# Sums out of a PSUM bank placed one to two slots ahead of the bank's next use, and token sums of a pair begun with its first block

## The chip, the cores and the metric

The kernel runs on one core of one Trainium2 chip, in float32. The metric is device time in microseconds (us), the median over runs. A core has five engines with a queue each: TensorE (PE, matmuls, with PEld for loading weights), VectorE (DVE), ScalarE (ACT), GpSimd (POOL) and SyncE (SP), which here only issues transfers. Each engine works its own queue in order; semaphores make one engine wait for another.

## The reference

Two blocks, one after the other. The first is an attention with sketched features: queries and keys (4 batches x 4 heads x 1088 rows x 32) are each projected twice to 8 values, whose outer product gives 64 features; keys and values are summed into a 64x32 matrix, and queries are multiplied into it and divided by a denominator. Its output, brought to 4352 tokens x 128, is the input `x` of the second block:

```
gate = 1.0 / (1.0 + np.exp(-(x @ w_gate)))      # 4352x128 @ 128x1536
val  = x @ w_val                                # 4352x128 @ 128x1536
out  = gate * val @ w_out                       # 4352x1536 @ 1536x128
```

Most of the arithmetic is in the second block, and the change touches only that.

## The kernel before, in words

The tokens go in chunks: eight of 512 and a last one of 256. Per chunk the 1536 hidden columns go in twelve blocks of 128 (`NJ`); the last chunk takes two blocks at once, so it has six steps. Such a step is a *wave*, made by `w1`: eight matmuls into two PSUM banks for gate and value (`wave`, L477), then ACT takes the sigmoid (`sg`, L485). In the next step `glu` lets DVE multiply value and sigmoid to the hidden block `g` (L507). Two blocks make a pair, `pair`.

The second matmul multiplies `g` with `w_out`. Chunk 0 and the last chunk do it plainly (`w2`, L370). Chunks 1 to 7, where `fast(ci)` holds, use a Strassen-like scheme with seven products instead of eight on a pair (two blocks of 128 hidden columns by two halves of 256 tokens by two halves of 64 outputs). It needs sums of weights, `ws`, made once by GpSimd in two halves (`weight_sums`, the second half called in chunk 1 when its second wave is issued), and for each pair sums of tokens, `tsum` rows t0 to t3, made by GpSimd in `token_sums`.

The products accumulate over the six pairs of a chunk in two banks. `w2_a` puts four of the seven products, a matmul each, into the first bank, `acc0`, and `w2_b` the other three into the second, `acc1`; all are recorded at L339 as `prod`. The lower 64 partitions of each bank are called `lo`, the upper `hi`. After the last pair the outputs must be put together from both banks: ACT copies `hi` to SBUF (`other`, L401 and L435), and DVE adds `lo` and the copies into rows of a tile `res` (all recorded at L412, the line of the helper `add`). Then `res` is transposed in two halves (`turned`, L451) and stored. The sums, by the names of the code:

- first sums: first bank's `lo` plus the first copy, for two rows of `res`
- third: the other half of the first bank's `lo`, plus a row of `res`; after it the first bank is free
- fourth: a row of `res` less the second copy; reads no bank
- fifth and seventh: the two halves of the second bank's `lo`; after them the second bank is free
- last sums: rows of `res` with each other; read no bank

The order of the work is written by hand: the four compute engines run in the order in which the program issues their instructions. `slot` is the loop of that order. One turn of it is a *slot*: it calls `glu` for the wave before, runs the next entry of `moe["late"]` (one list of sums), runs the products that are due from `moe["todo"]`, and issues one wave. Products of a pair are due three slots (`w2_a`) and four slots (`w2_b`) after its second block. So with s the slot of a chunk's last `w2_a`, slot s+1 has the last `w2_b`, slot s+2 the first `w2_a` of the next chunk into the same first bank, and slot s+3 the first `w2_b` into the second. The late sums ran in slots s+1 (first), s+2 (third), s+3 (fourth, fifth, seventh) and s+4 (last sums), each ahead of the products of its slot and behind the `g` of that slot.

Attention work of batches 1 to 3 is placed between slots by number (`plan`, and calls before it): transposes of keys and queries (`kT`, `qT`, `kab`), feature products (`kp`, `qp`), sums (`z`, `zs`) on DVE, small matmuls on PE, and transfers by SP. What SP issues is not in the hand-written order.

Of the kernel before, what the change touches and what calls it, by code (L numbers as in the profile page):

```python
# [8 lines left out]
F32 = mybir.dt.float32  # L9
# [3 lines left out]
ALU = mybir.AluOpType  # L13
# [3 lines left out]
P = 128  # L17
# [3 lines left out]
def kernel(  # L21
# [12 lines left out]
    nc = tc.nc  # L34
# [20 lines left out]
    raw = ctx.enter_context(tc.tile_pool(name="raw", bufs=NJ // 2))  # L55
# [90 lines left out]
    HALF = TCH // 2  # L146
    ws = const.tile([P, 4, NJ // 2, 64], F32, tag="ws", name="ws")
    w_in = {}
# [130 lines left out]
    for c in range(2):  # L279
        rows = slice(64 * c, 64 * c + 64)  # L280
        nc.vector.tensor_reduce(
            out=m_col[rows, c],
            in_=ident[rows].rearrange("p (k j) -> p j k", j=R),
            axis=mybir.AxisListType.X,
            op=ALU.add,
        )
    for t, x in (
# [5 lines left out]
        out=e_sum,  # L293
# [13 lines left out]
    moe = {"sum": -1, "ci": 0, "w": 0, "n": 0, "ready": 0, "acc": None, "gate": None, "todo": [], "late": []}  # L307
# [14 lines left out]
        ):  # L322
            nc.gpsimd.tensor_tensor(out=out, in0=in0, in1=in1, op=op)

    def token_sums(g):
        t = raw.tile([P, 4, HALF], F32, tag="w_in", name="tsum")
        g1 = g[:, 0].rearrange("p (t x) -> p t x", t=2)
        nc.gpsimd.tensor_tensor(  # L328
            out=t[:, :2],
            in0=g.rearrange("p f (t x) -> p t f x", t=2)[:, 1],  # L330
            in1=g1,
            op=ALU.subtract,
        )
        nc.gpsimd.tensor_tensor(out=t[:, 2], in0=t[:, 1], in1=g1[:, 0], op=ALU.add)  # L334
        nc.gpsimd.tensor_tensor(out=t[:, 3], in0=t[:, 2], in1=g[:, 1, :HALF], op=ALU.subtract)  # L335
        return t

    def product(out, lhsT, rhs, start, stop):
        nc.tensor.matmul(  # L339
# [46 lines left out]
    fst = {}  # L386

    def w2_a(ci, i, g, t):
        if i == 0:
            moe["sum"] = ci  # L390
            fst["a"] = pso.tile([P, TCH], F32, tag="acc0", name="prod")
        lo, hi = fst["a"][:64], fst["a"][64:]
        w, first, last = w_sb[:, 2], i == 0, i == NJ // 2 - 1
        product(lo[:, :HALF], w[:, 2 * i, :64], g[:, 0, :HALF], first, last)
        product(hi[:, :HALF], w[:, 2 * i + 1, :64], g[:, 1, :HALF], first, last)
        product(lo[:, HALF:], ws[:, 3, i], g[:, 1, HALF:], False, last)
        product(hi[:, HALF:], ws[:, 1, i], t[:, 2], False, last)
        if last:
            e = fst["e"] = raw.tile([P, 2, 2, HALF], F32, tag="w_in", name="other")[:64]
            r = fst["r"] = raw.tile([P, 5, HALF], F32, tag="w_in", name="res")[:64]  # L400
            nc.scalar.copy(out=e[:, 0], in_=hi.rearrange("p (u x) -> p u x", u=2))  # L401

            def first_sums():
                add(ends(r, 1, 3), twice(lo[:, :HALF]), e[:, 0])

            def third():
                add(r[:, 2], lo[:, HALF:], r[:, 4])

            moe["late"] += [[first_sums], [third]]

    def add(out, in0, in1, op=ALU.add):
        nc.vector.tensor_tensor(out=out, in0=in0, in1=in1, op=op)  # L412

    def twice(x):
        return bass.AP(tensor=x.tensor, offset=x.offset, ap=[list(x.ap[0]), [0, 2], [1, HALF]])

    def ends(r, u, step):
        x = r[:, u]
        return bass.AP(
            tensor=x.tensor, offset=x.offset, ap=[list(x.ap[0]), [step * HALF, 2], [1, HALF]]  # L420
        )

    def w2_b(ci, i, g, t):
        if i == 0:
            fst["b"] = pso.tile([P, TCH], F32, tag="acc1", name="prod")
        lo, hi = fst["b"][:64], fst["b"][64:]
        w, first, last = w_sb[:, 2], i == 0, i == NJ // 2 - 1
        p5 = (lo[:, :HALF], ws[:, 0, i], t[:, 0], first, last)
        p4 = (hi[:, :HALF], w[:, 2 * i + 1, 64:], t[:, 3], first, last)
        p7 = ((hi if i % 2 else lo)[:, HALF:], ws[:, 2, i], t[:, 1], False, i >= NJ // 2 - 2)  # L430
        for p in (p4, p5, p7) if i % 2 else (p5, p4, p7):
            product(*p)
        if last:
            e, r = fst["e"], fst["r"]
            nc.scalar.copy(out=e[:, 1], in_=hi.rearrange("p (u x) -> p u x", u=2))  # L435
            o_sb = sbA.tile([P, 2, TCH // 32, 32], F32, tag="o_sb", name="o_sb")

            def fourth():
                add(r[:, 3], r[:, 4], e[:, 1, 0], op=ALU.subtract)

            def fifth():
                add(ends(r, 2, 2), twice(lo[:, :HALF]), ends(r, 2, 2))

            def seventh():
                add(r[:, 0], lo[:, HALF:], e[:, 1, 1])

            def last_sums():
                add(r[:, 3:5], r[:, 3:5], twice(r[:, 0]))

            def turned(d):  # L450
                nc.vector.transpose(  # L451
                    out=o_sb[:64, d].rearrange("p t x -> p (t x)"),
                    in_=r[:, 1 + 2 * d : 3 + 2 * d].rearrange("p u x -> p (u x)"),
                )

            def turn_store():
                turned(1)
                store(ci, lambda g4: o_sb[32 * (g4 % 2) : 32 * (g4 % 2) + 32, g4 // 2])

            moe["late"] += [[fourth, fifth, seventh], [last_sums], [lambda: turned(0)], [turn_store]]  # L460

    def w1():

        ci = moe["ci"]
        t0, tw = tok_chk[ci]
        jn = TCH // tw
        j0 = moe["w"] * jn
        wv = psm.tile([P, 2, TCH], F32, tag="wave", name="wave")

        tp = tw // 2 if ci == 0 and j0 == 0 else tw  # L470
        turn = (moe["w"] // 2) % 2
        for o in range(0, tw, tp):
            for which in range(2):
                for jj in range(jn):
                    for c in (0,) if ci == 0 else (1 - turn, turn):
                        d = slice(0, P) if ci == 0 else slice(64 * c, 64 * c + 64)
                        nc.tensor.matmul(  # L477
                            out=wv[d, which, jj * tw + o : jj * tw + o + tp],
                            lhsT=w_sb[:, which, j0 + jj, d],
                            rhs=xT[:, t0 + o : t0 + o + tp],  # L480
                            start=True,
                            stop=True,
                        )
        sg = sbG.tile([P, TCH], F32, tag="sg", name="sg")
        nc.scalar.activation(out=sg, in_=wv[:, 0], func=ACTF.Sigmoid)  # L485
        if ci == 0:
            if j0 == 1:
                narrow_01(2, 3)
            if 0 < j0 < NJ - 2:
                narrow_w(j0 + 1, 3)  # L490
            narrow_w(j0 + 2, 1)
            narrow_w(j0 + 2, 2)
            if j0 < 3:
                narrow_w(j0 + 3, 0)
            if j0 > 1:
                narrow_w(j0 + 4, 0)
            if j0 == NJ - 3:
                weight_sums(0, NJ // 4)
        if ci == 1 and j0 == 1:
            weight_sums(NJ // 4, NJ // 2)  # L500
        if moe["w"] % 2 == 0:
            moe["g"] = sbG.tile([P, 2, TCH], F32, tag="g", name="g")
        pair, odd, n = moe["g"], moe["w"] % 2, moe["n"]

        def glu():
            g = pair[:, odd]
            nc.vector.tensor_tensor(out=g, in0=wv[:, 1], in1=sg, op=MUL)  # L507
            todo = moe["todo"]
            if not fast(ci):
                lag = 2 if ci == 0 else 3 if j0 else 4  # L510
                part = (ci, j0, jn, g.rearrange("p (j t) -> p j t", j=jn))
                todo.append((n + lag, lambda: w2(*part)))
            elif odd:
                part = (ci, j0 // 2, pair, token_sums(pair))
                todo.append((n + 3, lambda: w2_a(*part)))
                todo.append((n + 4, lambda: w2_b(*part)))

        moe["gate"] = glu
        moe["w"] += 1
        moe["n"] += 1  # L520
        if j0 + jn == NJ:
            moe["ci"] += 1
            moe["w"] = 0
# [6 lines left out]
    def slot(group, waves):  # L530

        if group is not None:
            group()
        todo = moe["todo"]
        for _ in range(waves):
            more = moe["ci"] < len(tok_chk)
            if more and sum(tok_chk[moe["ci"]]) > moe["ready"]:
                break
            glu()
            for step in moe["late"].pop(0) if moe["late"] else ():  # L540
                step()
            while todo and todo[0][0] <= moe["n"]:
                todo.pop(0)[1]()
            if more:
                w1()
            elif not todo:
                break
            else:
                todo.pop(0)[1]()
# [512 lines left out]
    else:  # L1062
        nc.vector.tensor_copy(
            out=s4[:, 1:],
# [8 lines left out]
        out=st_[:, : 2 * R],  # L1073
# [10 lines left out]
        out=sk,  # L1084
# [6 lines left out]
        op=MUL,  # L1091
# [75 lines left out]
    late = []  # L1167
# [122 lines left out]
```

## Time and profile before

| What | us |
|---|---|
| median of 3 runs | 337.98 |
| lowest and highest | 337.73, 340.97 |
| span of the profiled execution | 340.6 |
| PE busy on `wave` (L477) | 218.3 |
| PE busy on `prod`, four groups at L339 | 65.8 + 35.2 + 26.3 + 25.0 |
| DVE busy on `g` (L507) | 70.0 |
| POOL busy on `tsum` (L328, L334, L335) | 63.1 + 32.5 + 33.0 |

Busy times of PE overlap between groups, since matmuls are pipelined; the sum over groups is more than the engine's 301.0 us. The page cuts the span into 40 slices of 8.5 us and gives each engine's busy share in tenths. Idle time of an engine other than the bounding one costs nothing by itself.

### The profile page before, as it was taken

The numbers are of one execution on the slowest core, as the hardware profiler recorded it, in microseconds if no ns is written. First come the engines' busy times: TensorE is split into PE (matmuls) and PEld (weight loads), VectorE is DVE, ScalarE is ACT, GpSimd is POOL, SyncE is SP. The second block draws the span as 40 slices with busy tenths as digits, with TensorE's granted clock in tenths as the row PEclk, the third lists the DMA queues.
The fourth block names the chain that finished last, engine by engine and source line by source line (L and its number), as shares of the span: only waits on it lengthen the run. The fifth ranks groups of instructions, "written<-read, shape, count | busy, mean of one in ns | idle before, by whom it ended". The sixth has DMA issues, their size and how long they took to land.

```text
span 340.6 us, 5502 instructions
## 1 busy us (share of the span) xinstructions
PE 301.0 (88%) x2176; PEld 158.3 (46%) x2176; DVE 187.4 (55%) x317; ACT 88.8 (26%) x164; POOL 155.7 (46%) x178
## 2 busy tenths in 40 slices
PE   9899998999949997699977998599976997699973
PEld 4534332445524553246634554245633554256842
DVE  6987899865453674357534955247223423243333
ACT  3465422122312223022231224021221223022310
POOL 1565564843633455144452975334560654245300
PEclk9999999999998999899999999989997999899999
DMA  8985135654000665131006630001000200001003
GB/s 223 368 238 135 34 119 147 161 138 140 0 0 2 155 164 133 36 113 17 0 2 152 166 64 2 0 4 30 0 0 2 32 2 0 0 13 20 0 2 46
DMA packets 29689, 24.34 MB, mean 71 GB/s; under 512 B 19616, under 2 KB 24864, under 8 KB 29664
## 3 DMA queue, kind: packets, MB, share of 16 engines
q1 hardware_dynamic: 28752, 23.23, 26.3%
q10 hardware_dynamic: 912, 0.77, 0.9%
q8 instruction: 17, 0.28, 0.4%
q14 instruction: 8, 0.07, 0.1%
HBM read 20.73 MB, written 3.26 MB: 70 GB/s over the span
## 4 chain that ended last, share of the span: by engine, by line
PE 73%; DVE 9%; DMA 8%; POOL 4%; ACT 3%; issue 2%; SPq 1%; DVEq 0%; POOLq 0%
PE wave L477 47%; PE prod L339 19%; DVE g L507 3%; DVE res L412 3%; PE moeout L370 3%; ACT sg L485 3%; DMA v<-in_v_dram 3%; DMA w_in<-in_moe_w_out_dram 2%; DMA bq<-dq 2%; POOL tsum L328 2%; DMA w_in<-in_moe_w_gate_dram 1%; PE nps L1004 1%; POOL head L118 1%; PE kvz L810 1%; POOL tsum L334 1%
## 5 line engine op out<-in xcount | busy, mean ns | idle before, releaser
L477 PE MATMUL wave<-xT,w_sb 128*64 128x512 f32 (+3 forms) x820 | 218.3, 582 | 0.0
L507 DVE TENSOR_TENSOR g<-wave,sg 128x512 f32<-128x512 f32 x102 | 70.0, 687 | 135.7 <-ACT sg L485 135.7
L328 POOL TENSOR_TENSOR tsum<-g 128x512 f32<-128x512 f32 x42 | 63.1, 1503 | 133.2 <-DVE g L507 133.1
L485 ACT ACTIVATE sg<-wave 128x512 f32<-128x512 f32 x102 | 60.9, 597 | 223.8 <-PE wave L477 216.9
L477 PEld LDWEIGHTS wave<-xT,w_sb 128*64 128x64 f32 (+1 forms) x820 | 88.2, 143 | 66.7 <-issue 46.4
L339 PE MATMUL prod<-tsum,ws 128*64 128x256 f32 x252 | 65.8, 392 | 18.9 <-DVE res L412 17.3
L339 PEld LDWEIGHTS prod<-tsum,ws 128*64 128x64 f32 x252 | 31.7, 140 | 36.9 <-issue 26.2
L339 PE MATMUL prod<-g,w_sb 128*64 128x256 f32 x168 | 35.2, 392 | 11.0 <-DVE res L412 11.0
L335 POOL TENSOR_TENSOR tsum<-tsum,g 128x256 f32<-128x256 f32 x42 | 33.0, 785 | 3.3
L334 POOL TENSOR_TENSOR tsum<-tsum,g 128x256 f32<-128x256 f32 x42 | 32.5, 774 | 3.3
L339 PEld LDWEIGHTS prod<-g,w_sb 128*64 128x64 f32 x168 | 16.9, 142 | 32.3 <-issue 30.0
L339 PE MATMUL prod<-tsum,w_sb 128*64 128x256 f32 x84 | 26.3, 396 | 0.0
L339 PE MATMUL prod<-g,ws 128*64 128x256 f32 x84 | 25.0, 379 | 0.0
L118 POOL TENSOR_TENSOR head<-head,tail 128x384 int32<-128x384 int32 (+2 forms) x14 | 13.4, 955 | 18.1 <-DVE head L109 13.9
L370 PE MATMUL moeout<-g,w_sb 128*128 128x512 f32 (+1 forms) x48 | 18.6, 500 | 2.2 <-DVE res L412 1.8
L339 PEld LDWEIGHTS prod<-g,ws 128*64 128x64 f32 x84 | 11.5, 137 | 3.9
L370 PEld LDWEIGHTS moeout<-g,w_sb 128*128 128x128 f32 x48 | 8.5, 189 | 9.9 <-issue 6.1
L339 PEld LDWEIGHTS prod<-tsum,w_sb 128*64 128x64 f32 x84 | 11.0, 140 | 2.9 <-issue 2.3
L668 DVE TENSOR_TENSOR kp<-kab 128x1152 f32<-128x1152 f32 (+2 forms) x10 | 10.7, 1088 | 0.0
L788 DVE TENSOR_TENSOR qp<-qp,bq 128x1152 f32<-128x1152 f32 (+1 forms) x7 | 9.0, 1291 | 2.0 <-DMA bq<-dq 2.0
L451 DVE STREAM_TRANSPOSE o_sb<-res 64x512 f32<-64x512 f32 x14 | 9.6, 688 | 0.0
L127 DVE SCALAR_TENSOR_TENSOR w_sb<-square,head 128x384 f32<-128x384 f32 (+1 forms) x11 | 5.7, 518 | 3.9 <-POOL head L118 3.9
(110 smaller groups left out, 186.6 us busy)
## 6 DMA issues: line engine op xcount, KB each, us to landing
qp<-dq SPq DMA_DIRECT2D x7, 576.0 KB, 5.0
bq<-dq SPq DMA_DIRECT2D x14, 288.0 KB
v<-in_v_dram SPq DMA_DIRECT2D x16, 144.0 KB, 2.7
kq<-in_k_dram SPq DMA_DIRECT2D x3, 544.0 KB
kq<-in_q_dram SPq DMA_DIRECT2D x3, 544.0 KB
w_in<-in_moe_w_out_dram SPq DMA_DIRECT2D x6, 256.0 KB
w_in<-in_moe_w_gate_dram SPq DMA_DIRECT2D x5, 256.0 KB, 5.8
w_in<-in_moe_w_val_dram SPq DMA_DIRECT2D x5, 256.0 KB, 6.3
```

What stands on the lines that cost most here:

```text
L118: nc.gpsimd.tensor_tensor(out=head, in0=head, in1=tail, op=ALU.add)
L328: nc.gpsimd.tensor_tensor(out=t[:, :2], in0=g.rearrange("p f (t x) -> p t f x", t=2)[:, 1], in1=g1, op=ALU.subtract,)
L334: nc.gpsimd.tensor_tensor(out=t[:, 2], in0=t[:, 1], in1=g1[:, 0], op=ALU.add)
L335: nc.gpsimd.tensor_tensor(out=t[:, 3], in0=t[:, 2], in1=g[:, 1, :HALF], op=ALU.subtract)
L339: nc.tensor.matmul(out=out, lhsT=lhsT, rhs=rhs, start=start, stop=stop, skip_group_check=True)
L370: nc.tensor.matmul(out=moe["acc"][:, :tw], lhsT=w_sb[:, 2, j, :], rhs=g[:, jj, :tw], start=(j == 0), stop=(j == NJ - 1),)
L412: nc.vector.tensor_tensor(out=out, in0=in0, in1=in1, op=op)
L451: nc.vector.transpose(out=o_sb[:64, d].rearrange("p t x -> p (t x)"), in_=r[:, 1 + 2 * d : 3 + 2 * d].rearrange("p u x -> p (u x)"),)
L477: nc.tensor.matmul(out=wv[d, which, jj * tw + o : jj * tw + o + tp], lhsT=w_sb[:, which, j0 + jj, d], rhs=xT[:, t0 + o : t0 + o + tp], sta ...
L485: nc.scalar.activation(out=sg, in_=wv[:, 0], func=ACTF.Sigmoid)
L507: nc.vector.tensor_tensor(out=g, in0=wv[:, 1], in1=sg, op=MUL)
L668: eng.tensor_tensor(out=KP[b][:, pi, j0:j1].rearrange("p j m (i l) -> p (j m) i l", i=R), in0=bass.AP(tensor=a0.tensor, offset=a0.offset, ...
```

## The change

The sums that read a PSUM bank are placed one or two slots earlier relative to the slot in which the next chunk's products enter that bank, and those that read only SBUF are moved behind them. In the slots counted from s as above:

- the first sums are issued at once in slot s, right after the last `w2_a` and its copy
- third runs in slot s+1
- fifth and seventh run in slot s+2; two of the terms are now combined in another order, so `res` gets a sixth row
- fourth and the last sums, which read SBUF alone, run in slot s+3, and the two transposes follow in s+4 and s+5
- the last chunk's first block is due 3 slots after its wave as the others, no longer 4

The token sums of a pair are begun with its first block: t0 (a difference within the first block) is made then, and t2, t3, t1 after the second. One instruction on 512 columns and two on 256 become four on 256. The row that `w2_a` reads, t2, is the first of those after the second block.

```diff
-    def token_sums(g):
-        t = raw.tile([P, 4, HALF], F32, tag="w_in", name="tsum")
-        g1 = g[:, 0].rearrange("p (t x) -> p t x", t=2)
-        nc.gpsimd.tensor_tensor(
-            out=t[:, :2],
-            in0=g.rearrange("p f (t x) -> p t f x", t=2)[:, 1],
-            in1=g1,
-            op=ALU.subtract,
-        )
-        nc.gpsimd.tensor_tensor(out=t[:, 2], in0=t[:, 1], in1=g1[:, 0], op=ALU.add)
-        nc.gpsimd.tensor_tensor(out=t[:, 3], in0=t[:, 2], in1=g[:, 1, :HALF], op=ALU.subtract)
-        return t
+    def token_sums(g, t, odd):
+        def sub(u, in0, in1):
+            nc.gpsimd.tensor_tensor(out=t[:, u], in0=in0, in1=in1, op=ALU.subtract)
+
+        if not odd:
+            sub(0, g[:, 0, HALF:], g[:, 0, :HALF])
+            return
+        sub(2, g[:, 1, HALF:], t[:, 0])
+        sub(3, t[:, 2], g[:, 1, :HALF])
+        sub(1, g[:, 1, HALF:], g[:, 0, HALF:])
...
-            def first_sums():
-                add(ends(r, 1, 3), twice(lo[:, :HALF]), e[:, 0])
-
-            def third():
-                add(r[:, 2], lo[:, HALF:], r[:, 4])
-
-            moe["late"] += [[first_sums], [third]]
+            add(ends(r, 1, 3), twice(lo[:, :HALF]), e[:, 0])
+            moe["late"] += [lambda: add(r[:, 2], lo[:, HALF:], r[:, 4])]
...
-            def fourth():
+            def fifth_seventh():
+                add(ends(r, 2, 3), twice(lo[:, :HALF]), ends(r, 2, 2))
+                add(r[:, 0], lo[:, HALF:], e[:, 1, 1])
+
+            def last_sums():
                 add(r[:, 3], r[:, 4], e[:, 1, 0], op=ALU.subtract)
-
-            def fifth():
-                add(ends(r, 2, 2), twice(lo[:, :HALF]), ends(r, 2, 2))
-
-            def seventh():
-                add(r[:, 0], lo[:, HALF:], e[:, 1, 1])
-
-            def last_sums():
-                add(r[:, 3:5], r[:, 3:5], twice(r[:, 0]))
+                add(r[:, 3:5], ends(r, 3, 2), twice(r[:, 0]))
...
-            moe["late"] += [[fourth, fifth, seventh], [last_sums], [lambda: turned(0)], [turn_store]]
+            moe["late"] += [fifth_seventh, last_sums, lambda: turned(0), turn_store]
...
-                lag = 2 if ci == 0 else 3 if j0 else 4
+                lag = 3 if ci else 2
...
-            elif odd:
-                part = (ci, j0 // 2, pair, token_sums(pair))
+                return
+            if not odd:
+                moe["t"] = raw.tile([P, 4, HALF], F32, tag="w_in", name="tsum")
+            token_sums(pair, moe["t"], odd)
+            if odd:
+                part = (ci, j0 // 2, pair, moe["t"])
```

## The prediction

> **What bounds the kernel now.** I read first the busy shares, then the slices, then who waited for whom on TensorE, and last one stretch in order of time.
>
> ```profile
> span 340.6 us, 5502 instructions
> PE 301.0 (88%) x2176; PEld 158.3 (46%) x2176; DVE 187.4 (55%) x317; ACT 88.8 (26%) x164; POOL 155.7 (46%) x178
> ...
> PE   9899998999949997699977998599976997699973
> ...
> PEclk9999999999998999899999999989997999899999
> ```
>
> PE is the bound, busy 301.0 of 340.6 us. The reader is to see single low digits in the PE row at regular distances, and dips of the clock row beside them. 39.6 us are idle; the waits on PE say in front of what:
>
> ```profile
> PE prod L339 <- DVE res L412: 28.2, 12, 3.0
> PE moeout L370 <- DVE res L412: 1.8, 1, 1.8
> PE prod L339 <- POOL tsum L334: 1.6, 2, 1.2
> ```
>
> Columns: us in total, times, longest. So 30.0 us stand before the first matmul into a reused bank, released by the VectorE sums out of it. With 1.6 us behind GpSimd, about 2.4 us of start and about 5.4 us of drain after the last matmul that is all idle time of PE. One of six transitions between chunks, in order of time:
>
> ```profile
> 248.67 2.07 PE L477 MATMUL wave<-xT,w_sb 128*64 128x512 f32 x8
> 249.08 0.58 ACT L435 COPY other<-prod 64x512 f32<-64x512 f32 x1
> ...
> 249.76 0.67 DVE L412 TENSOR_TENSOR res<-prod,other 64x512 f32<-64x512 f32 x1
> 250.77 0.60 ACT L485 ACTIVATE sg<-wave 128x512 f32<-128x512 f32 x1 [1.11 <-PE wave L477]
> 251.40 0.69 DVE L507 TENSOR_TENSOR g<-wave,sg 128x512 f32<-128x512 f32 x1 [0.97 <-ACT sg L485]
> 252.01 0.41 DVE L412 TENSOR_TENSOR res<-prod,res 64x256 f32<-64x256 f32 x1
> ...
> 252.56 0.65 PE L339 MATMUL prod<-g,w_sb 128*64 128x256 f32 x4 [1.83 <-DVE res L412]
> ...
> 257.78 0.41 DVE L412 TENSOR_TENSOR res<-prod,other 64x256 f32<-64x256 f32 x1
> ...
> 258.33 0.66 PE L339 MATMUL prod<-tsum,ws 128*64 128x256 f32 x1 [2.96 <-DVE res L412]
> ```
>
> The sum that frees a bank (252.01) stands in VectorE's order behind the `g` of the wave that PE has just finished (wave, sg, g, sum), in the very slot whose products need that bank. PE pays the whole chain: 1.83 us for the first bank, 2.96 us for the second, where three sums queue. Last, the clock by stretches:
>
> ```profile
> 101.00:104.00 3.00, 2.88 (x11) 1.61 (x13) 0.66 (x1) 0.00 (x0) 0.00 (x0) 0.50 0.03 5
> 265.00:285.00 20.00, 20.00 (x125) 11.71 (x123) 6.75 (x10) 5.38 (x10) 11.53 (x13) 1.00 0.09 14
> ```
>
> The two numbers after the stretch are its length and PE's busy time; the third from the end is the granted clock. Right after the 2.96 us stall that ends at 101.12 it is 0.50; away from transitions PE has no gap and 1.00.
>
> **What the Trainium skill says.** "TensorE: Matmul & The Clock Gate", Part 1, puts the array at half clock after an idle window of about 3.4 us and has it return after about as much busy time; its closing table says to keep gaps under about 3 us. The trace roughly agrees: stalls of 2.96 us were enough five times of six, the 2.47 us one was not. "Perfetto Trace Analysis", Optimizing Tensor Performance, wants matmul groups to rotate over PSUM banks so that evacuation overlaps the next group; here two banks rotate but the evacuation is placed too late to overlap. "SBUF — State Buffer", Who interferes with whom, says a VectorE instruction with two SBUF inputs contends with GpSimd reading SBUF; the trace agrees, the 128x512 token difference took 1.27 us alone and 2.92 us beside the product `kp`.
>
> **The change part by part.** Let T be the end of the last products into the first bank, at the top of a slot, and use the steady rows of the chain: wave 1.72, first-bank products 0.86, second-bank products 0.65.
>
> First sums, moved into the slot of those products. The ACT copy begins 0.3 after T (its wait in the trace) and lasts 0.58; the sum 0.67: done at T+1.6. Queued behind it are that slot's `g`, wanted at T+1.72+0.65 = T+2.4, and at four transitions one attention operation (a 1.30 us transpose, a 1.2 to 1.34 us `qp` product, a 0.76 us transpose). The worst, T+1.6+1.34 = T+2.9, delays `g` by 0.5 us; its wave buffer is next wanted at T+1.72+0.65+1.72+0.86 = T+5.0. Cost on the path: nothing.
>
> Third sum, one slot after first. It follows that `g`: normally T+2.4+0.65+0.41 = T+3.5, at worst T+4.0. PE wants the first bank after wave, second-bank products and wave, T+4.1. Removed: 6 x 1.83 us, worst margin about 0.
>
> Fifth and seventh, one slot earlier. With W the end of the wave before: `g` starts at W+0.72, fifth 0.61 later, seventh 0.61 after that, and PE is released 0.55 later (257.78 to 258.33), W+2.49. PE wants the second bank after 0.86 and 1.73 us, at W+2.59. Removed: the other waits, margin 0.1 us. Together the 28.2 us.
>
> Fourth and the last sums move to the next slot and read SBUF alone; no bank waits for them. The sixth row of `res` has no time of its own.
>
> The lag of the last chunk's first block falls from 4 to 3. Its products then stand in the slot of the third sum, behind the second-bank products: the wait is 1.83 - 0.65 = 1.2 us, and 0.65 us is won.
>
> Clock. The stretches of 20 us with a clock under 1 are 0.91 four times, 0.95 and 0.97: 4 x 1.8 + 1.0 + 0.6 = 8.8 us of full-speed work lost. Without a stall near 3 us it comes back. Cross-check: second-bank start to second-bank start is 294.73 - 258.33 = 36.40 us; eight steady slots are 285.42 - 265.64 = 19.78 us, so twelve 29.67. A transition costs 6.73 = 4.8 of waits + 1.9 of clock. Five of these and one without the slow clock (about 4.5) give 38; the direct sum is 28.2 + 8.8 = 37.0, which I use.
>
> Token sums. One 128x512 and two 128x256 operations (1.27 + 0.73 + 0.73 = 2.73 us) become four 128x256 (2.92 us) per pair, against about 4.94 us of PE work per pair: GpSimd stays off the path. The row needed first, t2, comes after one operation behind the second `g` instead of two (2.0 us to 0.73). That should take the two waits of 1.6 us away. At chunk 1 the second half of the weight sums (four at about 0.6 us) now stands behind the first difference, but `g` for that is ready at 51.7 us and PE asks near 58.7.
>
> Drain. The last chunk's transpose no longer has a `res` transpose and its stores behind it. SP issues six stores in 3.11 us now; two could start earlier: 0.5 us.
>
> Sum: 28.2 + 0.65 + 8.8 + 1.6 + 0.5 = 39.8 us; 338.0 - 39.8 = 298.2. The profiled run was at 342.4 us against 338.0, so ordinary runs may have had fewer slow-clock episodes and less to regain (an estimate: up to 3 us), which I take in with 0.8 us: 299.
>
> **The rivals.** (a) Margins of 0 to 0.1 us fail, at attention transitions above all, since any VectorE delay goes straight into the wait. Short waits of about 0.5 us come back at most banks (12 x 0.5 = 6 us), too short to slow the clock: 305. For: DVE is 55% busy and its order is strict. Against: two of six transitions have no attention work at all. (b) The waits go but the clock does not recover, because it falls for another reason: 338 - 31 = 307. Against: 1.00 over 265 to 285 us with PE gapless. (c) The early first sum blocks VectorE on its copy, `g` and so waves and token sums come late, and GpSimd, 4.75 of 5 us busy at 186 to 191, becomes the bound: two new stalls of 3 us per transition, as long as those removed, and 338 to 342. Against: `g` has 2.6 us of room and the copy is done 0.9 us after the products.
>
> **How the numbers follow.** Forecast 72%, (a) 18%, (b) 6%, (c) 4%. The range runs from 295 (all regained, and the 338 run lost more than the stretches show) to 306, over (a). Faster by over 1% holds in all but (c): 0.96; within 1% 0.02, slower 0.02.
>
> **What would show it.** PE waits on res near 1 us in all where 30.0 stood; a clock of 1.00 in every stretch; PE at about 97% with nearly unchanged matmul rows; chunk to chunk 29.7 us; no PE wait on tsum. A wait of 0.3 us or more on second-bank products would say that the seventh sum is still late (a); a low clock without stalls (b); idle PE behind g or tsum (c).

## The result and the profile after

The changed kernel takes 300.24 us in the median (300.02 to 302.6, 4 runs) against 338.16 us before (337.73 to 340.97, 4 runs): a ratio of 0.8879, 95% interval 0.8813 to 0.8944. The forecast was 299.0 us. Ratios and intervals, here and below, leave out runs that took over 1.5% more than the fastest of their kernel.

The page of the changed kernel, its busy shares and two rows of its slices:

```profile
span 298.2 us, 5583 instructions
...
PE 289.7 (97%) x2176; PEld 152.4 (51%) x2176; DVE 186.9 (63%) x317; ACT 88.8 (30%) x164; POOL 161.0 (54%) x220
...
PE   8899999999999999999999999999999999999893
...
PEclk9999999999999999999999999999999999999998
```

The same 2176 matmuls, but PE is busy for 97% of the span instead of 88%; the low digits at regular distances are gone from its row and the dips from the clock row. PE's busy time itself fell by 11.3 us with the work unchanged, mostly since matmuls at half clock had counted as busy (the clock's share was put at 8.8 us): a kernel below that keeps six of the stalls, but at full clock, has 289.7 as well. Who waited for whom on PE (us in total, times, longest):

```profile
PE moeout L368 <- DVE res L405: 1.4, 1, 1.4
...
PE ndps L859 <- ACT kvd L825: 0.4, 1, 0.4
```

Of 30.0 us behind `res` only the wait at the last chunk is left, 1.4 us where the working had left 1.2, and PE waits no more on `tsum`. A transition in order of time, as the one shown of before:

```profile
219.47 0.68 DVE L405 TENSOR_TENSOR res<-prod,other 64x512 f32<-64x512 f32 x1 [0.20 <-ACT other L399]
...
221.25 0.69 DVE L496 TENSOR_TENSOR g<-wave,sg 128x512 f32<-128x512 f32 x1 [1.09 <-ACT sg L474]
221.86 0.41 DVE L405 TENSOR_TENSOR res<-prod,res 64x256 f32<-64x256 f32 x1
...
222.48 0.65 PE L337 MATMUL prod<-g,w_sb 128*64 128x256 f32 x4
...
223.37 0.69 DVE L496 TENSOR_TENSOR g<-wave,sg 128x512 f32<-128x512 f32 x1 [1.11 <-ACT sg L474]
223.98 0.67 DVE L405 TENSOR_TENSOR res<-prod,res 64x512 f32<-64x512 f32 x1
...
224.57 0.41 DVE L405 TENSOR_TENSOR res<-prod,other 64x256 f32<-64x256 f32 x1
...
225.13 0.40 PE L337 MATMUL prod<-tsum,ws 128*64 128x256 f32 x1
```

First sums at 219.47, third at 221.86, and the first bank's products enter at 222.48 without a wait in brackets. The second bank is read until 224.98 (224.57 + 0.41) and its next products start at 225.13, 0.15 us later. Before, with PE standing in wait, it was 0.14 us (258.19, the end of the read, to 258.33). So the bank comes free just in time, with nothing to spare. In the chain of the changed kernel second-bank products start at 225.28 and again at 255.03 us: 29.75 us from chunk to chunk, where it was 36.40.

### The profile page after: what moved, and what is told of

It reads as the page before. It is cut to its first block, busy times and chain, and to the rows that moved or that the text cites. A ratio compares the mean times of both kernels' runs of the same rounds, so it can differ in the third digit from the quotient of the medians.

```text
span 298.2 us, 5583 instructions
## 1 busy us (share of the span) xinstructions
PE 289.7 (97%) x2176; PEld 152.4 (51%) x2176; DVE 186.9 (63%) x317; ACT 88.8 (30%) x164; POOL 161.0 (54%) x220
## 4 chain that ended last, share of the span: by engine, by line
PE 84%; DMA 7%; DVE 4%; POOL 2%; issue 1%; SPq 1%; ACT 0%; POOLq 0%; DVEq 0%; ACTq 0%
PE wave L466 54%; PE prod L337 21%; PE moeout L368 3%; DMA v<-in_v_dram 3%; DMA w_in<-in_moe_w_out_dram 2%; POOL head L118 2%; DMA w_in<-in_moe_w_gate_dram 2%; PE nps L997 1%; PE kvz L803 1%; DVE w_sb L127 1%; DVE head L109 1%; DVE head L105 1%; PE kps L582 1%; PE cqps L728 0%; DVE qp L781 0%
## 5 line engine op out<-in xcount | busy, mean ns | idle before, releaser
L466 PE MATMUL wave<-xT,w_sb 128*64 128x512 f32 (+3 forms) x820 | 211.1, 566 | 0.0
L466 PEld LDWEIGHTS wave<-xT,w_sb 128*64 128x64 f32 (+1 forms) x820 | 84.2, 140 | 65.6 <-issue 49.4
L327 POOL TENSOR_TENSOR tsum<-g 128x256 f32<-128x256 f32 x84 | 66.8, 798 | 24.6 <-DVE g L496 24.4
L327 POOL TENSOR_TENSOR tsum<-g,tsum 128x256 f32<-128x256 f32 x42 | 35.1, 836 | 64.2 <-DVE g L496 64.0
L337 PE MATMUL prod<-tsum,ws 128*64 128x256 f32 x252 | 62.3, 381 | 0.0
L337 PEld LDWEIGHTS prod<-tsum,ws 128*64 128x64 f32 x252 | 30.9, 136 | 16.7 <-issue 12.6
L327 POOL TENSOR_TENSOR tsum<-tsum,g 128x256 f32<-128x256 f32 x42 | 32.8, 780 | 3.3
L337 PEld LDWEIGHTS prod<-g,w_sb 128*64 128x64 f32 x168 | 15.9, 136 | 19.1 <-issue 15.7
L337 PE MATMUL prod<-tsum,w_sb 128*64 128x256 f32 x84 | 25.4, 384 | 0.0
L405 DVE TENSOR_TENSOR res<-prod,other 64x512 f32<-64x512 f32 (+1 forms) x14 | 7.6, 544 | 3.1 <-DMA a<-dq 1.9
```

The costliest lines, as they stand in the source:

```text
L327: nc.gpsimd.tensor_tensor(out=t[:, u], in0=in0, in1=in1, op=ALU.subtract)
L337: nc.tensor.matmul(out=out, lhsT=lhsT, rhs=rhs, start=start, stop=stop, skip_group_check=True)
L466: nc.tensor.matmul(out=wv[d, which, jj * tw + o : jj * tw + o + tp], lhsT=w_sb[:, which, j0 + jj, d], rhs=xT[:, t0 + o : t0 + o + tp], sta ...
```

## Experiments

The theory is the prediction's: the placement removes the waits, and with the long waits goes a loss of clock; the token sums are a small part. The rivals give the gain to the token sums, or hold that stalls cost only their own length. Medians are compared with the 300.24 and 300.49 us that the changed kernel took in two sets of runs (300.4 below).

**The placement alone**: the old `token_sums` and its call are put back into the changed kernel (the diff in part).

```diff
-        sub(2, g[:, 1, HALF:], t[:, 0])
-        sub(3, t[:, 2], g[:, 1, :HALF])
-        sub(1, g[:, 1, HALF:], g[:, 0, HALF:])
+        t = raw.tile([P, 4, HALF], F32, tag="w_in", name="tsum")
...
+        nc.gpsimd.tensor_tensor(out=t[:, 2], in0=t[:, 1], in1=g1[:, 0], op=ALU.add)
```

> The changed kernel with the token sums of before (three GpSimd operations after the second block), the new placement of the res sums kept. Theory (the placement carries nearly all): only the waits behind GpSimd come back, 1.6 us in before, so about 302 us, clock near 1.00, no PE wait on res apart from the last chunk's 1.4. Rival (the token sums are needed once PE has no gaps, as t2 is ready 1.3 us later): waits on tsum at the stretches with attention sums, 304 us or more.

302.80 us, ratio 0.8915 (0.8876 to 0.8953). So the placement carries all but some 2.4 us. Its waits on PE:

```profile
PE moeout L370 <- DVE res L407: 1.4, 1, 1.4
PE prod L339 <- POOL tsum L334: 1.2, 1, 1.2
```

1.2 us of the 2.4 are the wait on `tsum` near 59.9 us. Against a repeated run of the changed kernel its waves fall behind by another 1.0 us between 174 and 181 us and by 0.4 us near 194 us. Just ahead of both places VectorE has attention work and GpSimd's sums are stretched (a 128x512 to 2.32 us from 1.27, a 128x256 to 1.72 from 0.73). That PE waits for these sums is likely, but the profile lists only a small part of it as waits.

**The token sums alone**, put into the kernel before:

> The kernel before with the new token sums alone, the res sums where they were. Theory: the 30 us of waits on res stay and 1.6 us of waits on tsum go: about 336.5 us. Rival (the earlier token sums carry part of the 38 us): 333 us or less.

338.41 us in the median of all 20 runs (332.81 to 342.63), against 340.79 in 23 runs of the kernel before; the seven runs that the ratio counts have 336.47, against 340.71 in 21. The ratio is 0.9869 (0.9817 to 0.992), a difference under 2%. The number of slow-clock episodes varies from run to run in both kernels, so I compare runs of the same mean granted clock: at 0.979 this kernel took 337.82 to 339.45 us and the one before 340.71 to 341.24, at 0.984 it took 336.47 to 337.04 against 339.56 to 339.79. So the token sums bring 2 to 3 us, a little more than the 1.6 expected. The waits on `res` stand as they were, 28.3 us in 12 times and 1.8 us in one, and PE no longer waits on `tsum`. The rival that gives them a large part falls, though the fastest of the 20 runs was at 332.81 us.

**Token sums in the new order, but not begun with the first block**:

```diff
         if not odd:
-            sub(0, g[:, 0, HALF:], g[:, 0, :HALF])
             return
+        sub(0, g[:, 0, HALF:], g[:, 0, :HALF])
```

> The changed kernel with all four token sums made after the second block, in the order t0, t2, t3, t1; the placement of the res sums is kept. t2 comes 0.73 us later than in the changed kernel, 0.6 us earlier than in the old form. Theory (the token sums matter only beside attention work of VectorE, and the form and the early begin share the 2.6 us that the old form cost): 300.5 to 302 us, with small waits on tsum near 59 us. Rival (only the order, t2 first, counts): 300.3 us, no wait.

300.31 us (300.14 to 300.75), ratio 0.8824 (0.879 to 0.8859): no difference from the changed kernel, as the rival had it. So the order counts: that t2 comes after two short operations instead of a long and a short one is enough; beginning with the first block buys nothing that can be measured here.

**The second bank late again**, at first in the order that it had before, with fourth ahead of fifth and seventh in slot s+3 (the diff in part; the empty entry holds the list back by a slot):

```diff
-            moe["late"] += [lambda: add(r[:, 2], lo[:, HALF:], r[:, 4])]
+            moe["late"] += [lambda: add(r[:, 2], lo[:, HALF:], r[:, 4]), lambda: None]
...
-            def fifth_seventh():
+            def fourth_fifth_seventh():
+                add(r[:, 3], r[:, 4], e[:, 1, 0], op=ALU.subtract)
```

> The changed kernel with fourth, fifth and seventh back in slot s+3, in that order, as before; the first bank is still freed early. Theory (a stall of 2.96 us also costs clock): six waits of 2.96 us = 17.8, plus about 1.8 us of slow clock at most of them: 326 to 328 us, clock under 0.95 in stretches. Rival (stalls cost only their own length): 318 us and a clock of 1.00 throughout.

326.17 us, ratio 0.9587 (0.9534 to 0.964): 25.8 us more than the changed kernel. The waits account for 16.6:

```profile
PE prod L337 <- DVE res L405: 16.6, 6, 2.8
```

Most of the other 9.2 us are clock: the mean granted clock of its four runs is 0.971 to 0.978, which is 7 to 9 us of work at full speed, against at most 1.2 us in the changed kernel. A stretch of this kernel with a transition in it (third from the end: granted clock):

```profile
240.00:260.00 20.00, 17.15 (x95) 9.12 (x93) 7.50 (x13) 3.58 (x6) 9.50 (x13) 0.91 0.09 14
```

**The first bank late again**, the second early:

```diff
-            add(ends(r, 1, 3), twice(lo[:, :HALF]), e[:, 0])
-            moe["late"] += [lambda: add(r[:, 2], lo[:, HALF:], r[:, 4])]
+            fst["third"] = third
+            moe["late"] += [first_sums]
...
             def fifth_seventh():
+                third()
```

> The changed kernel with the first sums back in slot s+1 and third in s+2, directly ahead of fifth and seventh; the last chunk's first block has lag 4 again, which this order needs. The second bank is free early. Theory: six waits of 1.83 us, and 0.4 us more at the last chunk: about 311.6 us, the clock stays at 1.00 since these stalls are short. Rival (any stall at a transition drops the clock): about 320 us with clock dips as in before.

312.61 us, ratio 0.9199 (0.9159 to 0.9238): 12.2 us more.

```profile
PE prod L337 <- DVE res L412: 11.0, 6, 1.8
PE moeout L368 <- DVE res L412: 1.8, 1, 1.8
```

11.0 plus the 0.4 us by which the last chunk's wait grew are 11.4 of the 12.2, and the clock keeps its level where a stall falls into a stretch:

```profile
260.00:280.00 20.00, 18.17 (x111) 10.04 (x108) 9.40 (x15) 4.76 (x8) 11.50 (x16) 1.00 0.09 14
```

So two kinds of stall, six times each at the same six transitions, cost 0.8 us or 9.2 us beyond their own length. Three more runs shortened the second bank's stall step by step, to see whether its length decides or which bank it stands at. With fifth and seventh late by the same empty entry, and without fourth ahead of them:

> The changed kernel with fifth and seventh back in slot s+3 but without fourth ahead of them: the stall at the second bank is about 0.44 us shorter than with fourth (2.8 measured there), some 2.35 us, six times. Theory (the clock drops only after a stall close to 3 us; the one of 2.47 us in before did not): 300.3 + 14 = 314 to 316 us, clock 0.99 or more. Rival (already 2.35 us is long enough): about 323 us with clock dips and a spread of several us between runs.

With fifth early, and fourth and seventh late:

```diff
-            moe["late"] += [fifth_seventh, last_sums, lambda: turned(0), turn_store]
+            moe["late"] += [fifth, fourth_seventh, last_sums, lambda: turned(0), turn_store]
```

> The changed kernel with fourth and seventh alone in slot s+3, fifth stays in s+2: a stall at the second bank of about 1.8 + 0.44 = 2.25 us, six times. Theory (the length of a stall decides on the clock, and the limit lies between the 1.83 us that did not lower it and the 2.4 us that did): either all runs near 300.4 + 13.5 = 314 us with a clock of 1.00, and the limit is above 2.25 us, or 320 to 324 us with dips, and it is below. Rival (the clock falls with any stall at the second bank, whatever its length): 320 us or more here and in the run with seventh alone.

With seventh alone late, fourth after it:

> The changed kernel with seventh alone in slot s+3: a stall at the second bank of about 1.8 us, as long as the first bank's in the run with first and third late. Theory (length decides, not which bank): 300.4 + 6 x 1.8 = 311 us, clock 1.00, little spread. Rival (the second bank's stall is what lowers the clock): 318 us or more, with dips.

| Late sums | longest stall, us | waits on `res` beyond the changed kernel's, us | median, us (ratio, interval) | over 300.4, us | beyond the waits, us | dips in the trace |
|---|---|---|---|---|---|---|
| first and third | 1.83 | 11.4 | 312.61 (0.9199, 0.9159 to 0.9238) | 12.2 | 0.8 | 0 |
| seventh | 1.91 | 11.0 | 313.34 (0.9232, 0.9185 to 0.9279) | 12.9 | 1.9 | 0 |
| fourth, seventh | 2.25 | 13.0 | 320.59 (0.9418, 0.9353 to 0.9483) | 20.2 | 7.2 | 2 |
| fifth, seventh | 2.51 | 14.6 | 325.42 (0.9547, 0.949 to 0.9604) | 25.0 | 10.4 | 5 |
| fourth, fifth, seventh | 2.85 | 16.6 | 326.17 (0.9587, 0.9534 to 0.964) | 25.8 | 9.2 | 5 |

Waits and dips (stretches of half clock at a transition) are those of the one profiled execution, medians those of four. The trace with fourth and seventh late prices both apart. From one second copy (`other`) to the next the changed kernel takes 29.78 us. Here a transition without a dip takes 32.18, that is 2.40 for a listed wait of 2.25, and one with a dip 33.85, that is 1.7 more. So a stall costs some 0.15 us more than the profile lists, six of them 0.9 us, and a dip 1.7 us. With five dips that makes 9.4 us beyond the waits, where 10.4 and 9.2 were measured. With seventh alone, the rest of its 1.9 us is a longer drain in that trace, 5.7 us against 4.6.

The expectation for fifth and seventh was wrong: I had put the limit near 3 us, and stalls of 2.51 us lower the clock nearly as much as those of 2.85. The slices of that run show it:

```profile
span 324.6 us, 5586 instructions
...
PEclk9999999999997999989997999999997999799999
```

With seventh alone late the stall is at the second bank too and costs little beyond itself, so the rival that blames the bank falls. Length decides whether a dip can come; what decides whether it does come is in the last section. At 2.25 us two of six transitions show the dip and the rest none (this run also waited 1.7 us for a transfer, a part of its 7.2):

```profile
span 318.9 us, 5586 instructions
...
PEclk9999999999999999979999999999997999999998
...
PE denj L934 <- DMA b<-dq: 1.7, 2, 1.3
```

**The margin at the second bank**, beside a repetition of the changed kernel on the same chip:

> The changed kernel once more, as the yardstick of the next three on the same chip. Every theory expects 300 to 301 us with little spread, since no stall near 3 us is left that could cost clock in one run and not in the next; the kernel before should spread over several us.

300.49 us (299.73 to 301.42), ratio 0.8811 (0.8766 to 0.8856); the kernel before went from 337.54 to 342.53 us there. Then fourth was put ahead of fifth and seventh, in slot s+2:

> The changed kernel with one thing undone: fourth, which reads no bank, is again ahead of fifth and seventh, now in slot s+2. Theory (the second bank comes free with a margin of 0 to 0.1 us): 0.44 us more of VectorE ahead of the release at six transitions, so six PE waits of 0.35 to 0.45 us and 2.1 to 2.6 us more than the changed kernel. Rival (there is room of half a us): no PE wait on res there and no difference.

302.62 us (301.46 to 304.6), ratio 0.8874 (0.8826 to 0.8923): 2.1 us more in the median, though the intervals overlap. Its trace has the wait that theory expects, half as long as expected:

```profile
PE prod L337 <- DVE res L405: 0.9, 5, 0.2
```

And by the start of the last chunk's first `moeout`, 283.46 against 281.74 us in the repetition, the six transitions took 1.7 us more, five of them 0.34 us each and one nothing. Fourth holds VectorE up by 0.33 us there (224.82 to 225.15, where fifth starts), less than the 0.44 expected, and all of it reaches PE: the read of the bank ends at 226.16 and its products start at 226.31. So the second bank had no room at these five transitions, and the trace shows that it paid to split fourth off; the medians alone would not.

**The lag of the last chunk**: 4 again for its first block.

> The changed kernel with the last chunk's first block due after 4 slots again. Theory: the 1.4 us wait of PE on third at the last chunk comes from the lag of 3, as the products stand in third's own slot; with 4 they come one slot later and the wait goes: 1.4 us less than the changed kernel, about 299. My prediction's working held the lag of 3 for a gain of 0.65 us over before; the rival by that working is 0.65 us or more above the changed kernel.

299.71 us (298.24 to 300.76), ratio 0.8778 (0.8727 to 0.8829). The wait on `res` is gone from the trace as expected. The gain of 0.8 us in the median can't be told from nothing by the intervals, and the profiled run lost 1.1 us near 74 us in waits for a transfer that have nothing to do with the lag. The traces are clearer: from the last second copy to the end of the last matmul it is 12.9 us in the repetition of the changed kernel, 12.9 in the kernel before, and 11.1 here and again in the next run. So with the new placement the lag of 3 costs 1.8 us of PE's time, and against before it wins nothing.

With half of the stores of the last full chunk on ScalarE's queue as well:

> As the one with lag 4, and half of the stores of the last full chunk are issued by ScalarE, as those of the last chunk are. Theory: SyncE's four issues ahead of the last two stand in 2.99 us of queue at the end, two fewer save 0.5 to 1 us of the drain: about 298.2. Rival (the drain is the latency of the last transfer alone): no difference from lag 4.

298.98 us (297.9 to 302.15), ratio 0.8775 (0.8724 to 0.8827). From the end of the last transpose (293.88 us in the repetition, 292.45 here) to the end of the span it was 4.1 us and 4.0 us: the queue is not what the drain waits for. This is the lowest median of all, but by the intervals it is not shown to be faster than the changed kernel.

## Why the prediction was right, point by point

- **The waits of 28.2 us.** Right in mechanism, and nearly in size: placing the sums took all twelve away, and putting either bank's sums back brought its six back at 1.83 or 2.85 us. They were worth about 30.4 us, since a stall costs more than its listed wait: in the run with the token sums alone, a transition without a dip takes 34.95 us from second copy to second copy (282.67 to 317.62) against 29.78, so 5.17 for waits of 1.83 + 2.96 = 4.79. Five such transitions and one with the shorter stall, 4.6, make 30.4.
- **The clock, 8.8 us.** Right in mechanism, shown by the pair of late banks, and right in size for the profiled execution alone: its five dips of 3.41 us at half clock are 8.5 us. The ordinary runs had fewer. Runs of before at 337.35 to 337.83 us, about as long as its median, had a mean clock of 0.989 to 0.990, those near 342.4 us 0.974: 3.7 us lost against 8.9, or two dips against five. So the medians could regain about 3.4 us (an estimate; the clock of the runs behind the 338.16 is not on record). The working also took the limit to be near 3 us from one stall of 2.47 us without a dip; 2.02 us has been enough.
- **The second bank's margin of 0.1 us.** There was none. The products start 0.15 us after the last read, the time that a release took before as well, and 1.78 us after the first matmul of the wave ahead of them where it is 1.72 in the steady rows. What is lost is some 0.06 us, so the waits of 0.5 us that the rival expected did not come about.
- **The lag of the last chunk, 0.65 us won.** Wrong. The wait went from 1.8 to 1.4 us, but the time from the last second copy to the last matmul stayed at 12.9 us, and the old lag with the new placement has no wait there and takes 11.1. I compared with the wait of before and did not see that the early third sum removes it by itself.
- **The token sums, 1.6 us.** Right for the waits on `tsum`; taking the new form out cost 2.4 us, 0.8 more than priced. The reason was partly wrong, since the early begin does nothing and the earlier t2 does it.
- **The rivals.** (a) came within 0.1 us at the second bank, as above. (b) fell: in the profile after the clock is full up to the last matmul. (c) fell: PE waits on neither `g` nor `tsum`.
- **The drain, 0.5 us.** From the last matmul's end (chain: 335.20 before, 293.60 after) to the end of the span it is 5.4 and 4.6 us: 0.8.
- **The number, 299.0 against 300.24.** It is closer than its terms. I subtracted 39.8 us and added 0.8 for runs that had lost less clock than the profiled one; the medians differ by 37.9, the two profiled spans by 42.4. Redone with what the runs showed the sum is 30.4 + 0 + 3.4 + 2.4 + 0.8 = 37.0. The clock's term, 8.0 after the allowance, was some 4.6 us too large, because the profiled execution of before, at 342.37 us, was one of its long ones; the stalls and the token sums were some 3 us too small. That the two errors nearly cancel is luck.

## What to carry to other kernels

Where two PSUM banks alternate between groups, ask for each bank which instruction reads it last and what stands ahead of that on its engine in the slot where the bank is wanted again; a short sum behind a long dependency (wave, sigmoid, product) costs the whole chain. Free the bank a slot earlier and move work that reads only SBUF behind it. Price a stall on TensorE with its length and, from about 2 us upward, with up to 1.7 us of slow clock as well, which some executions pay and others do not. Before pricing what the clock gives back, compare the granted clock of the profiled execution with that of the median run. And count what a second edit to the same wait still has to remove.

## What the runs showed of the hardware that was not expected

Whether a stall brings a dip of the clock depends on where it falls. Every dip before the drain lasts 3.41 us at a clock of 0.50, and within a trace dips start whole multiples of 3.413 us apart: in the kernel before at 100.90, 141.86, 220.37, 257.92 and 295.46 us, that is 12, 23, 11 and 11 steps. If each trace is cut into stretches of 3.41 us on that grid, all 20 dips of the 14 traces follow a stretch in which PE was idle for 2.02 us or more, and no stretch with 2.01 us or less is followed by one (from 12 us to the last matmul; where a trace has no dip, the grid is that of the low clock at its end; PE's ends are modelled, so the limit is one of the profile's idle time). The prediction, with the page on the clock gate that it names, had an idle window of about 3.4 us; in these traces 2.02 us of idle time within such a stretch were enough.

Two cases, with PE's busy time after the length and the clock third from the end. The first two rows are of the run with fifth and seventh late, where a stall of 2.02 us lies in one stretch; the other three of the token sums alone, where one of 2.96 us (138.49 to 141.45) is divided by a boundary:

```profile
170.50:173.91 3.41, 1.39 (x36) 0.63 (x22) 2.34 (x5) 1.15 (x2) 1.73 (x3) 1.00 0.22 86
173.91:177.32 3.41, 3.41 (x13) 1.23 (x11) 0.00 (x0) 0.00 (x0) 0.00 (x0) 0.50 0.41 105
...
136.31:139.73 3.42, 2.18 (x13) 0.70 (x9) 0.48 (x1) 0.60 (x1) 1.27 (x2) 1.00 0.00 0
139.73:143.14 3.41, 1.69 (x11) 1.05 (x13) 2.81 (x5) 0.00 (x0) 0.83 (x1) 1.00 0.02 5
143.14:146.55 3.41, 3.41 (x23) 1.84 (x21) 1.28 (x2) 0.60 (x1) 0.83 (x1) 1.00 0.73 226
```

So stalls of 1.91 us never brought one, those of 2.96 us five of five times in the kernel before but two of five with the token sums alone, and the number of dips in the table is a matter of where the stalls fell; the longer one is, the more of the places give a dip. No run moved a stall of one length across the grid on purpose, and what sets the limit near 2.0 us is not shown. The number of dips also sets most of the spread between runs of the kernel before, 337.52 to 342.57 us in 21 runs, against 299.73 to 302.6 us in 10 runs of the changed one.

The last sums, two SBUF inputs of 64x512, took 0.67 us before and 1.10 us at five of seven places after the change. There the GpSimd operation had started first; at the other two no GpSimd operation ran beside them and they took 0.68:

```profile
226.81 0.83 POOL L327 TENSOR_TENSOR tsum<-g 128x256 f32<-128x256 f32 x1 [0.39 <-DVE g L496]
...
227.08 1.10 DVE L405 TENSOR_TENSOR res<-res 64x512 f32<-64x512 f32 x1
```

With fourth ahead of fifth and seventh in slot s+2 the same two came in the other order:

```profile
227.49 0.67 DVE L405 TENSOR_TENSOR res<-res 64x512 f32<-64x512 f32 x1
227.65 1.10 POOL L327 TENSOR_TENSOR tsum<-g 128x256 f32<-128x256 f32 x1 [0.35 <-DVE g L496]
```

The one that starts second is stretched (GpSimd's 0.83 in the first pair stood behind fourth, which started at 226.64). "SBUF — State Buffer", Who interferes with whom, in the Trainium skill says that issue order and not the kind of operation decides who blocks, and these traces agree: 0.43 us for VectorE there, 0.37 us for GpSimd here (1.10 against 0.73 alone). No bank waits for the last sums, so it cost nothing.
